# q and k of a tile, and V of two tiles, side by side for each partition: transfers that fill 64 partitions with 4 KB rows

## The chip, the cores and the metric

The kernel runs on one core of a Trainium2 chip. The metric is the device time of one execution in microseconds (us); several executions are timed and their median is taken. One more execution is recorded by the hardware profiler, and everything below that speaks of rows, waits and the chain comes from that one.

The core's engines are named as the profile names them: PE (matrix multiplies), PEld (PE's weight loads), DVE (vector), ACT (scalar, activations), POOL (GpSimd) and SP (which only issues transfers here). SBUF is the on-chip memory of 128 partitions, PSUM the memory that PE writes. Transfers (DMAs) between the off-chip memory and SBUF are carried by 16 DMA engines.

## The reference

Block-diagonal attention on 8 batches, 8 heads, 576 positions and 64 values per head, in chunks of 64, followed by a mixture of experts in which each token that passes a gate goes to one of eight experts:

```python
q_c = q.reshape(B, H, nc, chunk, D)            # chunk = 64, k_c and v_c alike
scores = scale * np.matmul(q_c, k_c.transpose(0, 1, 2, 4, 3))
attn = np.exp(scores - np.max(scores, axis=-1, keepdims=True))
attn = attn / (np.sum(attn, axis=-1, keepdims=True) + 1e-09)
out = np.matmul(attn, v_c)
x = out.transpose(0, 2, 1, 3).reshape(B * S, H * D)      # 4608 tokens of 512 values
do_compute = x @ w_skip > 0
e_idx = argmax(x @ w_gate); gate = softmax(x @ w_gate)[e_idx]
result = x, and where do_compute: x + gate * (relu(x @ w1[e_idx]) @ w2[e_idx])
```

## The kernel before, in words

The 4608 tokens form 36 tiles (NT) of 128 tokens; a tile holds two chunks of all eight heads. The kernel has two stages. The first is the attention stage, a loop over `i` of 39 iterations (line 724 on) in which the steps of several tiles are interleaved by hand: in iteration `i` PE makes the scores of tile `i` (`pe_scores`, line 241), transposes the probabilities of tile `i - 2` (`pe_ptrans`, 273), multiplies those of tile `i - 3` with V (`pe_pv`, 289), transposes the result of tile `i - 4` (`pe_xt`, 316) and, every second iteration, makes the gate's logits of two tiles (`pe_logit`, 328). ACT copies PSUM to SBUF and takes exponentials, DVE takes the maxima and normalises, POOL subtracts. Beside these the routing of tokens to experts is counted, and the first expert's weights are loaded and split into two 16-bit parts. The second stage is the mixture of experts: rows are gathered by an indirect transfer from POOL, multiplied by two weight matrices and scattered back.

The transfers of the attention stage are all issued by SP, in the order in which the code names them. Three kinds bring the inputs:

- `load_q(t)` (line 126) and `load_k(t)` (129) each fill one half of the tile `st`, 128 partitions with 512 fp32 values each, so 2048 bytes a row and 256 KB a transfer. The inputs were laid out by the host so that these are whole blocks of memory.
- `load_v(t)` (133) fills a tile `sv`: 128 partitions, 520 values (2080 bytes) each, 260 KB. The values carry a column of ones that gives the softmax's sum.

The first five tiles of q and k (`QK_AHEAD`) and the first six of V (`V_AHEAD`) are loaded ahead of the loop. In iteration `i` the loop issues `load_q(i + 5)` right after the scores of tile `i`, then one transfer of `side` (line 304: a result tile written to `out`, line 310, or half a weight chunk `wst`, line 360), later `load_v(i + 3)` and `load_k(i + 5)`. There are five `st` buffers and six `sv` buffers, so `load_q(i + 5)` waits until PE has read tile `i`'s scores inputs, and `load_v(i + 3)` until PE has read V of tile `i - 3`.

Nobody plans this order at run time: within an engine the instructions stand as the code was recorded, and between engines semaphores hold. Each SP transfer uses one of eight completion semaphores in turn and waits for the transfer that used it before, so that at most eight SP transfers are under way.

Of the kernel before, what the change touches and what calls it, by code (L numbers as in the profile page):

```python
# [9 lines left out]
F32 = mybir.dt.float32  # L10
# [8 lines left out]
P = 128  # L19
B, H, S, D = 8, 8, 576, 64  # L20
CH = 64
NTOK = B * S
NT = NTOK // P
# [3 lines left out]
KC = DM // P  # L27
# [28 lines left out]
QK_AHEAD = 5  # L56
V_AHEAD = 6
# [46 lines left out]
def moe_attention_kernel(ctx: ExitStack, tc: tile.TileContext, qk: bass.AP, vo: bass.AP, cst: bass.AP, crow: bass.AP, wall: bass.AP, out: bass.AP):  # L104
    nc = tc.nc
# [8 lines left out]
    ap = apool.__enter__()  # L114
# [5 lines left out]
    T = [dict() for _ in range(NT)]  # L120
    lgs = {}
    halves = (slice(0, CH), slice(CH, P))

    def load_q(t):
        T[t]["st"] = ap.tile([P, 2, DM], F32, name="st", bufs=QK_AHEAD)
        nc.sync.dma_start(T[t]["st"][:, 0], qk[0, t])

    def load_k(t):
        nc.sync.dma_start(T[t]["st"][:, 1], qk[1, t])

    def load_v(t):
        T[t]["sv"] = ap.tile([P, 2 * KC, D + 1], F32, name="sv", bufs=V_AHEAD)
        nc.sync.dma_start(T[t]["sv"].rearrange("p h d -> p (h d)"), vo[t])

    man = tc.manual_schedule()
    man.__enter__()
    csb = cpool.tile([P, CCOLS], F32, name="csb")
    rsb = cpool.tile([1, RCOLS], F32, name="rsb")
    for t in range(QK_AHEAD):
        load_q(t)  # L140
        load_k(t)
        if t == 1:
            nc.sync.dma_start(csb, cst)
        if t == 2:
            nc.sync.dma_start(rsb, crow)
        if t >= 2:
            load_v(t - 2)
    for t in range(QK_AHEAD - 2, V_AHEAD):
        load_v(t)
# [8 lines left out]
    def pe_warm(n):  # L158
        for _ in range(n):
            nc.tensor.matmul(warm, ones, zeros, start=True, stop=True)  # L160
# [32 lines left out]
    def more_constants():  # L193
        nc.vector.tensor_copy(upper, C("upper"))
        nc.vector.tensor_copy(cbase, C("cbase"))
        nc.vector.tensor_copy(recs[:, 0:2], C("tok").rearrange("p (c t) -> p c t", c=2))
        nc.vector.tensor_copy(dcon, csb[:, _C["wdesc"][0]:_C["iota"][1]])
        nc.vector.memset(ecum[:, 0, :], 0.0)
        nc.vector.memset(onesf, 1.0)
# [28 lines left out]
    def fill(q, budget):  # L228
        while q and budget >= 0.5 * q[0][0]:
            c, _, f = q.pop(0)  # L230
            f()
            budget -= c
# [59 lines left out]
    def ve_x(t):  # L292
        xq = T[t].pop("xq")[:, :, :XW].rearrange("p a (j d) -> p a j d", j=KC)
        rr = spool.tile([P, 2, KC, 1], F32, name="rr", bufs=2)
        nc.vector.tensor_scalar(rr, xq[:, :, :, D:], 1e-9, None, op0=ALU.add)
        nc.vector.reciprocal(rr, rr)
        x = ap.tile([P, DM], F32, name="xa", bufs=X_BUFS)
        nc.vector.tensor_tensor(x.rearrange("p (j a d) -> p a j d", a=2, d=D), xq[:, :, :, :D], rr.to_broadcast([P, 2, KC, D]), op=ALU.mult)  # L298
        rows.append((t, x))
        T[t]["x"] = x  # L300
# [3 lines left out]
    def side(i, n):  # L304
        for _ in range(n):
            if pieces and (pieces[0] < FC and i in W_AT or i >= BURST and pieces[0] >= FC and (not rows or pieces[0] <= (i - BURST) * 2 + FC)):
                load_half(pieces.pop(0))
            elif rows:
                t, x = rows.pop(0)
                nc.sync.dma_start(out[t * P:(t + 1) * P, :], x)  # L310
# [52 lines left out]
    def conv_half():  # L363
        st, hi, lo = cws.pop(0)
        nc.scalar.activation(hi, st, AF.Copy, scale=SW)
        fd.append((600, None, lambda: nc.vector.scalar_tensor_tensor(lo, st, SW, hi, op0=ALU.mult, op1=ALU.subtract)))

    def pool_lo():
        hi, st, lo = pl.pop(0)
        nc.gpsimd.tensor_tensor(lo, st, hi, op=ALU.subtract)  # L370
# [271 lines left out]
    def on(f, t):  # L642
        if 0 <= t < NT:
            f(t)
# [26 lines left out]
    def stage(g):  # L671
        next(jobs[g])
# [27 lines left out]
    def u0_mm():  # L700
        fc, n = u0[0], units[0][3]
        u0[0] += 1
        hp = u0_bank(fc)[:, :n]
        for m, (a, b, j) in enumerate((a, b, j) for a, b in ((0, 0), (0, 1), (1, 0)) for j in range(KC)):
            nc.tensor.matmul(hp, wsets[0][:, a, fc, j * P:(j + 1) * P], xt0[:, b, j, :n], start=(m == 0), stop=(m == 11))
        u0_ev.append((hp, fc))

    def u0_out():
        l1_out(ht0, *u0_ev.pop(0), units[0][3])

    def early_xt():
        return [blk_xt(xt0[:, :, :, m * P:(m + 1) * P], xgs[m], xp=u0_bank(m)) for m in range(2)]

    def do(i, spot):
        for f, a in spots.pop((i, spot), ()):
            f(*a)

    def conv_pool():
        st, hi, lo = cws.pop(0)
        nc.scalar.activation(st, st, AF.Copy, scale=SW)  # L720
        nc.scalar.activation(hi, st, AF.Copy)
        pl.append((hi, st, lo))

    for i in range(NT + 3):
        on(pe_scores, i)
        on(load_q, i + QK_AHEAD)
        if i == 2:
            more_constants()
        wm = WARM[i + 1] if i + 1 < len(WARM) else (0, 0, 0, 0)
        pe_warm(wm[0])  # L730
        on(ve_max, i - 1)
        if i != NT + 1:
            on(ve_x, i - 4)
        side(i, 1 if i < BURST else 2)
        if i % 2 == 0:
            on(ve_logit, i - 8)
        do(i, "d")
        if i == NT + 1:
            for f in lows:
                f()  # L740
        fill(fd, 600)
        do(i, "p")
        pe_warm(wm[1])
        on(ac_scores, i)
        on(pe_ptrans, i - 2)
        on(ac_pt, i - 2)
        do(i, "m")
        on(ac_exp, i - 1)
        pe_warm(wm[2])
        while pl:  # L750
            pool_lo()
        for c in range(W_CONV.count(i)):
            conv_half() if i < NT - 2 else conv_pool()
        pe_warm(wm[3])
        on(pe_pv, i - 3)
        if i >= 3:
            on(load_v, i - 3 + V_AHEAD)
        on(load_k, i + QK_AHEAD)
        if i >= BURST:
            side(i, 2)  # L760
        if i == NT + 2:
            ve_x(NT - 1)
            stage(5)
        if i % 2 == 0:
            on(pe_logit, i - 6)
            on(ac_logit, i - 6)
        if i % 2:
            on(pe_ltrans, i - 7)
        on(pe_xt, i - 4)
        on(ac_xt, i - 4)  # L770
        do(i, "e")
        if i == NT:
            ve_x(i - 3)
            scpool.__exit__(None, None, None)
            upool = tc.tile_pool(name="ps_u", bufs=1, space=PSUM, reuse_waits="tile")
            ps_u = upool.__enter__()
            lows = early_xt()
        if i > NT:
            u0_mm()
        if u0_ev and i > NT + 1:  # L780
            u0_out()
# [214 lines left out]
def lay_out(q, k, v, moe_w_skip, moe_w_gate, moe_w1, moe_w2):  # L996
    nch = S // CH

    def cols(a):
        a = a.reshape(B, KC, 2, nch, CH, D).transpose(0, 3, 5, 1, 2, 4).reshape(NT, 2, D, KC, 2, CH).copy()  # L1000
        a[:, :, :, :, 1] = a[:, ::-1, :, :, 1]
        return a.reshape(NT, P, DM)

    vv = v.reshape(B, KC, 2, nch, CH, D).transpose(0, 3, 2, 4, 1, 5).reshape(NT, 2, P, KC, D).transpose(0, 2, 1, 3, 4)
    vo = np.ones((NT, P, 2, KC, D + 1), np.float32)
    vo[..., :D] = vv
    vo = vo.reshape(NT, P, 2 * KC * (D + 1))
    qk = np.ascontiguousarray(np.stack([cols(q), cols(k)]))
    cst, crow = constants()
    wsg = np.concatenate([moe_w_skip[:, None], moe_w_gate], axis=1)  # L1010
    lo, hi = _C["wsg"]
    wp = np.zeros((P, KC, WP), np.float32)
    wp[:, :, :NE + 1] = wsg.reshape(KC, P, NE + 1).transpose(1, 0, 2)
    cst[:, lo:hi] = wp.reshape(P, -1)
    w1 = moe_w1.reshape(NE, KC, P, FC, P).transpose(0, 3, 2, 1, 4).reshape(NE, FC, P, KC * P)
    w2 = moe_w2.reshape(NE, FC, P, DM)
    wall = np.ascontiguousarray(np.concatenate([w1, w2], axis=3))
    return {"in_qk": qk, "in_vo": vo, "in_cst": cst, "in_crow": crow, "in_wall": wall}
# [14 lines left out]
```

## Time and profile before

| what | value |
|---|---|
| median of 3 runs | 351.37 us (349.95 to 352.65) |
| the profiled execution's own time | 348.98 us |
| its span | 347.1 us |
| PE, DVE, ACT, POOL busy | 94%, 69%, 56%, 37% of the span |
| moved by DMA | 81.85 MB, 62.2% of the 16 engines' span in SP's queue |
| first and last score matmul | 5.7 and 118.5 us after the span's start |

The profile has several views. The page gives busy shares, the span in 40 equal slices (each digit is the busy share in tenths), the DMA queues, the chain of work that ended last and the costliest groups. The trace behind it can be asked for windows (busy time of each engine, the granted clock of PE, the mean busy share of the 16 DMA engines and the GB/s that they moved in a stretch of time), for waits (who waited for whom, total, how often, longest), for the chain of waits in order of time, and for a timeline. In a row of the timeline stand the start, the duration, the engine and line, the operation, the tile written and the tiles read, and a count. A packet is counted whole in the window in which it starts, so a share can come out a little above 1. "issue" means that the engine waited for nothing that the profile shows.

### The profile page before, as it was taken

What the parts mean: (1) busy time and instruction counts of PE and PEld (TensorE: products, weight loads), DVE (VectorE), ACT (ScalarE), POOL (GpSimd) and SP (SyncE); (2) the same over time, 40 slices, a digit from 0 to 9 for tenths busy, and PEclk for the clock granted to TensorE, in tenths of its full rate; (3) what the DMA queues carried; (4) which work ended last, traced back from release to release, by engine and by line L of the source; (5) the groups of instructions that cost most, each with busy time, mean ns of one, the idle gap of its engine ahead of it and who ended that gap; (6) DMA issues with size and microseconds to landing.
All of it is one profiled execution on the core that took longest, in us unless ns stands there. A gap on an engine that the chain in (4) does not pass through costs nothing.

```text
span 347.1 us, 10869 instructions
## 1 busy us (share of the span) xinstructions
PE 325.1 (94%) x4364; PEld 223.3 (64%) x4364; DVE 239.7 (69%) x534; ACT 194.7 (56%) x345; POOL 129.3 (37%) x158
## 2 busy tenths in 40 slices
PE   7699999998989899969999999999999999999991
PEld 3477777676767668638655555756756658678570
DVE  1545788876888787957787756966957948767430
ACT  2578889796778795414455633544634634636120
POOL 4523364543628466744143027316324222111111
PEclk9989999999999999999999999999999999999998
DMA  7999999999899981083558667668549667655000
GB/s 253 390 371 386 348 374 337 340 315 309 273 307 312 355 297 63 2 298 112 188 187 289 193 242 223 223 196 271 171 182 295 222 227 245 196 203 148 34 24 30
DMA packets 34407, 81.85 MB, mean 236 GB/s; under 512 B 4255, under 2 KB 4256, under 8 KB 34354
## 3 DMA queue, kind: packets, MB, share of 16 engines
q1 hardware_dynamic: 31250, 71.79, 62.2%
q0 software_dynamic: 3104, 9.33, 7.4%
q8 instruction: 36, 0.59, 0.7%
q14 instruction: 17, 0.14, 0.1%
HBM read 67.07 MB, written 14.17 MB: 234 GB/s over the span
## 4 chain that ended last, share of the span: by engine, by line
PE 79%; ACT 7%; DVE 5%; issue 4%; DMA 2%; POOL 2%; POOLq 0%; DVEq 0%; ACTq 0%
PE sp L544 26%; PE hp L519 23%; PE sc L241 7%; PE sp L316 5%; PE xq L289 4%; PE sp L273 4%; PE sp L328 3%; PE xt L502 2%; ACT sc L246 2%; ACT pz L278 2%; PE rk L160 2%; DMA xg<-out,rec3i 2%; PE xq L341 1%; POOL wset L370 1%; DVE x L552 1%
## 5 line engine op out<-in xcount | busy, mean ns | idle before, releaser
L544 PE MATMUL sp<-wset,ht 128*128 128x512 f16 (+7 forms) x528 | 104.0, 379 | 0.0
L519 PE MATMUL hp<-xt,wset 128*128 128x288 f16 (+6 forms) x768 | 85.8, 273 | 0.2 <-DVE ht L528 0.2
L519 PEld LDWEIGHTS <-wset 128*128 128x128 f16 x768 | 69.5, 98 | 17.3 <-issue 2.1
L544 PEld LDWEIGHTS <-ht 128*128 128x128 f16 (+7 forms) x528 | 46.6, 102 | 45.4 <-issue 1.7
L218 DVE SCALAR_TENSOR_TENSOR wset<-wst,wset 128x1024 f16<-128x1024 f32 x56 | 67.3, 1217 | 8.7 <-ACT wset L217 7.5
L221 POOL DMA_INDIRECT out<-x,recsi x18 | 23.6, 1310 | 112.9 <-DVE x L552 98.3
L253 POOL TENSOR_TENSOR px<-sc,mx 128x512 f32<-128x512 f32 x36 | 38.0, 1058 | 53.5 <-DVE mx L251 29.8
L217 ACT ACTIVATE wset<-wst 128x1024 f16<-128x1024 f32 x56 | 57.5, 1048 | 0.0
L527 ACT ACTIVATE ht<-hp 128x288 f16<-128x288 f32 (+6 forms) x64 | 24.4, 383 | 57.1 <-PE hp L519 56.0
L528 DVE SCALAR_TENSOR_TENSOR ht<-hp,ht 128x288 f16<-128x288 f32 (+6 forms) x64 | 26.0, 420 | 22.9 <-ACT ht L527 20.9
L251 DVE TENSOR_REDUCE mx<-sc 128x8 f32<-128x512 f32 x36 | 24.4, 678 | 19.0 <-ACT sc L246 18.5
L503 ACT ACTIVATE xt<-xt 128x512 f16<-128x512 f32 (+7 forms) x20 | 10.3, 513 | 47.5 <-PE xt L502 42.6
L241 PE MATMUL sc<-st 64*64 64x64 f32 x1152 | 27.3, 230 | 2.9 <-issue 2.1
L241 PEld LDWEIGHTS sc<-st 64*64 64x64 f32 x1152 | 21.9, 139 | 10.6 <-issue 6.3
L289 PE MATMUL xq<-sv,pz 64*64 64x65 f32 x1152 | 26.7, 228 | 1.9 <-issue 1.6
L246 ACT ACTIVATE sc<-sc 128x512 f32<-128x512 f32 x36 | 21.5, 597 | 11.2 <-PE sc L241 9.2
L289 PEld LDWEIGHTS xq<-sv,pz 64*64 64x64 f32 x1152 | 21.3, 137 | 8.7 <-issue 6.1
L273 PE MATMUL sp<-csb,px 128*128 128x128 f32 x144 | 24.0, 290 | 2.8 <-issue 2.8
L506 DVE SCALAR_TENSOR_TENSOR xt<-xt 128x512 f16<-128x512 f32 (+7 forms) x20 | 11.7, 585 | 21.4 <-ACT xt L503 18.2
L221 POOL DMA_INDIRECT xg<-out,recsi x18 | 24.3, 1352 | 5.5 <-issue 3.4
L322 ACT ACTIVATE xc<-sp 128x512 f32<-128x512 f32 x36 | 21.4, 595 | 8.1 <-PE sp L316 6.5
L298 DVE TENSOR_TENSOR xa<-xq,rr 128x512 f32<-128x512 f32 x36 | 24.9, 691 | 1.2
(156 smaller groups left out, 369.7 us busy)
## 6 DMA issues: line engine op xcount, KB each, us to landing
wst<-in_wall SPq DMA_DIRECT2D x56, 512.0 KB
st<-in_qk SPq DMA_DIRECT2D x72, 256.0 KB
sv<-in_vo SPq DMA_DIRECT2D x36, 260.0 KB
out<-xa SPq DMA_DIRECT2D x36, 256.0 KB
wst<-in_wall SPq DMA_DIRECT2D x16, 256.0 KB
csb<-in_cst SPq DMA_DIRECT2D x1, 312.5 KB
xg<-out,recsi POOLq DMA_INDIRECT x18
out<-x,recsi POOLq DMA_INDIRECT x18, 4.7
```

The costliest lines, as they stand in the source:

```text
L217: nc.scalar.activation(w[:, 0, fc, :], st, AF.Copy, scale=SW)
L218: nc.vector.scalar_tensor_tensor(w[:, 1, fc, :], st, SW, w[:, 0, fc, :], op0=ALU.mult, op1=ALU.subtract)
L221: ins = nc.gpsimd.indirect_dma_start(**kw)
L241: nc.tensor.matmul(sp[halves[c], a, j], st[halves[r], 0, w], st[halves[r], 1, w], start=(j == 0), stop=True, skip_group_check=True)
L246: nc.scalar.activation(sc.rearrange("p (j a) s -> p a j s", a=2), T[t].pop("sp"), AF.Copy)
L253: nc.gpsimd.tensor_tensor(px, T[t].pop("sc"), mx.unsqueeze(2).to_broadcast([P, H, CH]), op=ALU.subtract)
L273: nc.tensor.transpose(pt[:, j, :], px[:, j].rearrange("p a s -> p (a s)"), ident)
L289: nc.tensor.matmul(xq[w, a, j * (D + 1):(j + 1) * (D + 1)], pz[r, j, w], v[r, c, j], start=(j == 0), stop=True, skip_group_check=True)
L298: nc.vector.tensor_tensor(x.rearrange("p (j a d) -> p a j d", a=2, d=D), xq[:, :, :, :D], rr.to_broadcast([P, 2, KC, D]), op=ALU.mult)
L519: nc.tensor.matmul(hp, w()[:, a, fc, j * P:(j + 1) * P], xt[:, b, j, :n], start=(m == 0), stop=(m == 11))
L528: nc.vector.scalar_tensor_tensor(ht[:, 1, fc, :n], hp, 0.0, ht[:, 0, fc, :n], op0=ALU.max, op1=ALU.subtract)
L544: nc.tensor.matmul(y[c * P // cg:c * P // cg + n], ht[:, a, fc, o:o + n], w[:, b, fc, P * KC:], start=(f == 0 and m == 0), stop=(f == fw - ...
```

## The change

Nothing is computed otherwise. The host lays q and k of a tile side by side for each partition (1024 values, 4096 bytes), and V of tiles 2m and 2m + 1 side by side (1040 values, 4160 bytes). A transfer still moves 256 KB (260 KB for V), but now fills 64 of the 128 partitions with such rows: `load_qk0(t)` brings q and k of partitions 0 to 63, `load_qk1(t)` those of 64 to 127; `load_v(t)` brings, for an even `t`, V of tiles `t` and `t + 1` in partitions 0 to 63, and for an odd `t` the same two tiles' V in 64 to 127. The transfers stand at the same places of SP's order as the ones that they replace. V's six buffers of one tile become four of two tiles each (`V_AHEAD // 2 + 1`).

```diff
-    def load_q(t):
+    def load_qk0(t):
         T[t]["st"] = ap.tile([P, 2, DM], F32, name="st", bufs=QK_AHEAD)
-        nc.sync.dma_start(T[t]["st"][:, 0], qk[0, t])
-
-    def load_k(t):
-        nc.sync.dma_start(T[t]["st"][:, 1], qk[1, t])
+        nc.sync.dma_start(T[t]["st"][:P // 2], qk[t, :P // 2])
+
+    def load_qk1(t):
+        nc.sync.dma_start(T[t]["st"][P // 2:], qk[t, P // 2:])
 
     def load_v(t):
-        T[t]["sv"] = ap.tile([P, 2 * KC, D + 1], F32, name="sv", bufs=V_AHEAD)
-        nc.sync.dma_start(T[t]["sv"].rearrange("p h d -> p (h d)"), vo[t])
+        h = halves[t % 2]
+        if t % 2 == 0:
+            vp = ap.tile([P, 2, 2 * KC, D + 1], F32, name="sv", bufs=V_AHEAD // 2 + 1)
+            T[t]["sv"], T[t + 1]["sv"], T[t + 1]["vp"] = vp[:, 0], vp[:, 1], vp
+        else:
+            vp = T[t].pop("vp")
+        nc.sync.dma_start(vp[h].rearrange("p t h d -> p (t h d)"), vo[t // 2, h])
...
     for i in range(NT + 3):
         on(pe_scores, i)
-        on(load_q, i + QK_AHEAD)
+        on(load_qk0, i + QK_AHEAD)
...
         if i >= 3:
             on(load_v, i - 3 + V_AHEAD)
-        on(load_k, i + QK_AHEAD)
+        on(load_qk1, i + QK_AHEAD)
...
-    vo = vo.reshape(NT, P, 2 * KC * (D + 1))
-    qk = np.ascontiguousarray(np.stack([cols(q), cols(k)]))
+    vo = vo.reshape(NT // 2, 2, P, 2 * KC * (D + 1)).transpose(0, 2, 1, 3).reshape(NT // 2, P, 4 * KC * (D + 1)).copy()
+    qk = np.stack([cols(q), cols(k)], axis=2)
```

The diff adds five lines ahead of the rest, so that line 241 of the kernel before is line 246 after, and so on.

No engine's order changes but in shapes and waits. SP's queue in the first iterations of the loop, before: `st` is the tile of q and k, `sv` that of V, `xa` a result; DMAHW0 to DMAHW7 are the eight completion semaphores, and PE in a wait means that PE has to have read the buffer.

```order
L126 DMA st<-in_qk 128x512 [waits DMAHW0_49,PE_49]
L133 DMA sv<-in_vo 128x520 [waits DMAHW1_49,PE_49]
L129 DMA st<-in_qk 128x512 [waits DMAHW2_49]
L126 DMA st<-in_qk 128x512 [waits DMAHW3_49,PE_49]
L310 DMA out<-xa 128x512 [waits DMAHW4_49,DVE_49]
L133 DMA sv<-in_vo 128x520 [waits DMAHW5_49,PE_49]
```

The same place of SP's queue after:

```order
L126 DMA st<-in_qk 64x1024 [waits DMAHW0_49,PE_49]
L138 DMA sv<-in_vo 64x1040 [waits DMAHW1_49]
L129 DMA st<-in_qk 64x1024 [waits DMAHW2_49]
L126 DMA st<-in_qk 64x1024 [waits DMAHW3_49,PE_49]
L315 DMA out<-xa 128x512 [waits DMAHW4_49,DVE_49]
L138 DMA sv<-in_vo 64x1040 [waits DMAHW5_49]
```

The order stands; the shapes are 64 partitions by twice the columns, and V's transfers no longer wait for PE, since their buffer was last read an iteration earlier.

PE's queue where it makes scores, transposes probabilities and multiplies with V, from the scores of tile 5 on, before (`sc` are scores, `xq` is the product with V):

```order
L241 MATMUL sc<-st 64x64 [waits DMAHW3_49,DMAHW2_49,Activation_49]
L241 MATMUL sc<-st 64x64 x15
L273 MATMUL sp_405<-csb,px 128x128 [waits PE_49,Activation_49]
L273 MATMUL sp_405<-csb,px 128x128 x3
L289 MATMUL xq<-sv,pz 64x65 [waits DMAHW6_49,DVE_49,PE_49]
L289 MATMUL xq<-sv,pz 64x65 x15
```

And after:

```order
L246 MATMUL sc<-st 64x64 [waits DMAHW2_49,Activation_49]
L246 MATMUL sc<-st 64x64 [waits DMAHW3_49]
L246 MATMUL sc<-st 64x64 x14
L278 MATMUL sp_401<-csb,px 128x128 [waits PE_49,Activation_49]
L278 MATMUL sp_401<-csb,px 128x128 x3
L294 MATMUL xq<-sv,pz 64x65 [waits DMAHW6_49,DVE_49,PE_49]
L294 MATMUL xq<-sv,pz 64x65 [waits DMAHW7_49]
L294 MATMUL xq<-sv,pz 64x65 x14
```

Each score still waits for two transfers, now one after the other; the product with V of an even tile waits for two transfers where it waited for one, and that of the odd tile for none.

More of the change, by code (lines that the diff above doesn't have):

```diff
@@ L139, in moe_attention_kernel @@
     for t in range(QK_AHEAD):
-        load_q(t)
-        load_k(t)
+        load_qk0(t)
+        load_qk1(t)
         if t == 1:
```

## The prediction

> **What bounds the kernel now.** I read the page's slices first, then the stage that the change touches in windows of 10 us, then PE's waits and the chain in that stage. The slices (engines' busy tenths, DMA's, and GB/s):
>
> ```profile
> PE   7699999998989899969999999999999999999991
> ...
> DMA  7999999999899981083558667668549667655000
> GB/s 253 390 371 386 348 374 337 340 315 309 273 307 312 355 297 63 2 298 112 188 187 289 193 242 223 223 196 271 171 182 295 222 227 245 196 203 148 34 24 30
> ```
>
> A slice is 8.7 us. In the first 15, the attention stage, PE and the DMA engines are both full; nothing else of the kernel is touched. Two windows there (busy us of PE, PEld, DVE, ACT, POOL, then PE's clock, DMA share, GB/s):
>
> ```profile
> 20.00:30.00 10.00, 9.88 (x268) 7.58 (x266) 6.10 (x15) 8.37 (x15) 3.13 (x3) 0.99 1.03 374
> 30.00:40.00 10.00, 9.76 (x270) 7.31 (x270) 5.88 (x14) 8.65 (x17) 3.13 (x3) 1.00 1.03 375
> ```
>
> Which of the two is late? PE's waits, longest first and the last row (who waits, for whom, us in total, times, longest):
>
> ```profile
> PE xt L502 <- DMA xg<-out,rec3i: 3.2, 1, 3.2
> PE sp L273 <- issue: 2.8, 1, 2.8
> ...
> PE xq L289 <- PE sp L273: 0.2, 1, 0.2
> ```
>
> The one DMA that PE waits for is a gather of the second stage; no row names `st` or `sv`. The chain of waits repeats every two tiles with PE and ACT alone, which the transposition of the logits' inputs marks:
>
> ```profile
> 24.98 0.64 PE sp L328 x8
> ...
> 30.81 0.64 PE sp L328 x8
> ...
> 36.64 0.64 PE sp L328 x8
> ```
>
> So two tiles take 5.83 us of PE and ACT, 2.92 us each, and transfers just keep up. They have no room: a cheaper transfer shortens nothing, a dearer one soon shows.
>
> **Price of a transfer by its bytes.** A stretch with rows of 2 KB alone, and one of the second stage with the 4 KB rows of the weights alone, both over 128 partitions:
>
> ```profile
> 9.80:11.80 2.00, 1.97 (x53) 1.24 (x43) 1.29 (x3) 1.58 (x4) 1.32 (x2) 1.00 1.05 402
> 149.90:151.40 1.50, 1.50 (x11) 0.76 (x8) 1.27 (x4) 0.60 (x1) 0.33 (x1) 1.00 1.02 415
> ```
>
> GB/s by share is the rate of full engines: 402/1.05 = 383 and 415/1.02 = 407. 262,144 bytes then take 0.68 us now and 0.64 us with 4 KB rows: 0.04 us less for each. That is the whole gain, and the chain above does not contain it.
>
> **Price of filling half of the partitions.** No transfer of before fills 64 partitions. The nearest rows are the last scatters of expert rows from SBUF, one row of 2 KB for each partition, of 128, 104 and 112 rows (`BLOCKS`, line 50), issued by POOL
>
> ```profile
> 324.88 0.99 POOL L221 DMA_INDIRECT out<-x,recsi  x1 [11.05 <-DVE x L552]
> 331.55 1.02 POOL L221 DMA_INDIRECT out<-x,recsi  x1 [5.67 <-DVE ht L528]
> 341.48 0.96 POOL L221 DMA_INDIRECT out<-x,recsi  x1 [8.91 <-issue]
> ```
>
> with nothing else under way 1.6 us later, in the same order:
>
> ```profile
> 326.50:327.00 0.50, 0.50 (x4) 0.29 (x3) 0.23 (x1) 0.00 (x0) 0.00 (x0) 1.00 1.00 377
> 333.30:333.55 0.25, 0.25 (x7) 0.15 (x4) 0.25 (x2) 0.01 (x1) 0.00 (x0) 1.00 1.16 213
> 343.00:343.40 0.40, 0.00 (x0) 0.00 (x0) 0.00 (x0) 0.00 (x0) 0.00 (x0) 1.00 1.05 287
> ```
>
> Rates of full engines: 377 for 128 rows, 213/1.16 = 184 for 104, 287/1.05 = 273 for 112. Engines are as busy and move 2.05 and 1.38 times less. I read it so: over 128 partitions each engine has a way into SBUF of its own, and where the partitions are not all there, two engines are sent through one. That reading is an inference, these rows read SBUF where the change writes it, and they are short; but they are the only rows here in which partitions are missing.
>
> If 64 partitions give the 16 engines half of the ways, a transfer costs between 0.64 us (factor 1) and 1.32 us (factor 2.05). It need not be the whole factor, because the transfers alternate between lower and upper partitions: when one of two engines that share a way is ahead, it is already in the other half and both run freely. How far are they apart? The first transfer's first packets:
>
> ```profile
> 2.04:2.20 0.16, 0.16 (x2) 0.08 (x1) 0.00 (x0) 0.16 (x1) 0.16 (x2) 1.00 0.49 141
> 2.20:2.36 0.16, 0.16 (x2) 0.07 (x1) 0.00 (x0) 0.01 (x1) 0.16 (x1) 1.00 0.64 230
> 2.36:2.48 0.12, 0.12 (x1) 0.00 (x0) 0.00 (x0) 0.00 (x0) 0.12 (x1) 1.00 0.93 358
> ```
>
> Half of the engines start at 2.04 us, the rest by 2.48, on average about 0.28 us later. If the early and the late engine share a way and keep that lead, each transfer saves it: 1.32 - 0.28 = 1.04 us. I take that value, since full engines stay as far apart as they started; the ends 0.64 and 1.32 stay for the range.
>
> **Who must wait for it.** SP's issues up to the last one for q and k, of tile 35, by line (duration in ns, first and last start):
>
> ```profile
> L126 SPq DMA_DIRECT2D st<-in_qk x36: 327/328/975, 0.7 to 101.8; - x36
> L129 SPq DMA_DIRECT2D st<-in_qk x36: 328/441/1554, 1.2 to 103.4; - x36
> L133 SPq DMA_DIRECT2D sv<-in_vo x34: 327/328/1019, 4.4 to 103.0; - x34
> L310 SPq DMA_DIRECT2D out<-xa x19: 344/382/1917, 18.7 to 102.2; - x19
> L360 SPq DMA_DIRECT2D wst<-in_wall x8: 422/423/1572, 42.4 to 88.8; - x8
> L143 SPq DMA_DIRECT2D csb<-in_cst x1: 432/432/432, 2.6 to 2.6; - x1
> ```
>
> That is 36 + 36 + 34 = 106 transfers that change, 27 of 256 KB that don't (0.68 us each, 18.4) and the constants (312.5 KB, 0.8 us), from 2.0 us on. At a price P the last scores can start at 106 P + 18.4 + 0.8 + 2.0 = 106 P + 21.2. They start now at
>
> ```profile
> 118.04 0.68 PE L241 MATMUL sc<-st 64*64 64x64 f32 x29
> ```
>
> With P = 0.64 the transfers are through at 89 us, 29 us early. The point from which they decide is P = (118.0 - 21.2)/106 = 0.91. With 1.04 the scores start at 131.4, 13.4 us late. The same sum at tile 20, with 61 changed transfers and 12 others ahead of it in SP's order, and now
>
> ```profile
> 65.19 0.69 PE L241 MATMUL sc<-st 64*64 64x64 f32 x32
> ```
>
> gives 61 x 1.04 + 8.2 + 2.8 = 74.4 against 65.2, 9 us late: the delay builds up through the stage and is no matter of its end. After tile 35 the same work of PE follows as now, so the delay stays: **+13 us**.
>
> **The other edits.** V's transfer of an even slot no longer waits for PE; SP's waits on that line now:
>
> ```profile
> SPq L133 <- PE xq L289: 8.9, 13, 1.8
> ...
> SPq L133 <- PE xq L341: 4.2, 6, 1.1
> ```
>
> 13 us of SP's time go, but PE does not wait for V, so it is worth nothing; if engines are the bound, the wait for the transfer eight places earlier comes in its place. V of an even tile needs both halves, the second issued one iteration later. It is issued four iterations, about 12 us, before its use; at P = 1.04 eight transfers need 8.3 us. Nothing, then; without that cover it would be one transfer for each pair, 18 x 1.04 = 19 us at most. `load_qk1` adds no wait: q and k were both needed before. No instruction of PE, DVE, ACT or POOL is added.
>
> **Sum.** 348.98 us of the profiled execution + 13 = 362; the median lies 2.4 us above that execution, which is itself below the lowest of the three runs, so I say **363 us**.
>
> **The rivals.**
>
> *Ways are shared and no lead helps.* The engines drain, restart together, and lower and upper transfers run one after the other at half rate: P = 1.32, last scores at 161, +43 us, 394. For it: the full 2.05 of the 104 rows. Against: the spread at the start. [...] Chance 0.14.
>
> *The price stays under the point of 0.91.* Writes into SBUF may be taken in by something in between, so that a stretch of 0.6 us in the lower half is still written while the engine fills the upper, or the factor is the 1.38 of the 112 rows (P = 0.89). Then PE and ACT still set the pace, 349 to 353 us. For it: 29 us of room at P = 0.64, and rows that only show reads. Chance 0.32.
>
> *Faster.* Transfers do set the pace somewhere, for the share of 1.03 says so; each of 106 saves 0.04 us, 4 us in all, 345 us by the profiled execution, 347 by the median. It decides if P stays at 0.64 and the stretches that the profile names "issue" are late data. Against: no wait of PE for `st` or `sv`. Chance 0.10.
>
> **How the numbers follow.** The forecast, P from 0.95 to 1.2, has 0.44; its own range is +4 to +30 us, 355 to 381. A measurement of this kernel tells about 1% (3.5 us) from no change. Faster by more: the last rival and a little chance, 0.11. Within: the rival under the point and the weak end, 0.30. Slower: forecast and first rival, 0.59. The range runs from 346 to 384; it leaves out the first rival and the edge of the last, together under 0.2.
>
> **What would show it.** Right: waits of PE for `st` at line 246 of some 13 us together, DMA share still about 1.0 between 20 and 100 us but 260 to 300 GB/s instead of 374, last scores near 131 us, and the second stage as long as now. First rival: 200 to 230 GB/s and last scores near 160. Second: GB/s and the 5.83 us of two tiles unchanged. Third: shorter than 5.83 us. The forecast is wrong if the rate of full engines stays near 400 GB/s, or if the delay shows up without waits for `st` or `sv`.

## The result, and the profile after

The changed kernel takes 391.25 us (median of 4, 387.5 to 396.8) against 350.87 us; the ratio is 1.111 with a 95% interval of 1.101 to 1.121. It is 40 us slower, where 12 were forecast: outside the range, and three times the forecast. A few executions of each kernel come out longer than the rest (396.8 is one), and ratios compare the others.

The profiled execution took 387.5 us with a span of 385.7. The page's slices (9.6 us each) of the changed kernel:

```profile
PE   7748797867797697999699999999999999999992
...
DMA  7999999999999999620815587586755876675100
GB/s 187 221 228 254 291 330 244 254 259 257 242 239 232 271 327 360 247 83 2 306 26 206 184 294 215 175 286 188 220 207 184 298 237 206 213 229 190 44 24 27
```

The DMA engines are as full as before and for longer, but move 220 to 330 GB/s in most slices where they moved 270 to 390. Two windows of the changed kernel (PE, PEld, DVE, ACT, POOL, PE's clock, DMA share, GB/s):

```profile
20.00:30.00 10.00, 5.47 (x109) 4.25 (x109) 2.44 (x5) 3.12 (x6) 1.48 (x2) 0.80 1.04 230
...
60.00:70.00 10.00, 8.35 (x226) 6.31 (x228) 6.43 (x20) 6.84 (x14) 4.82 (x11) 1.00 1.04 244
```

The first of these stood at 374 GB/s with PE at 9.88 us busy. What PE waits for, in the changed kernel:

```profile
PE sc L246 <- issue: 10.1, 7, 2.7
PE xq L294 <- issue: 8.5, 5, 2.9
PE sc L246 <- DMA st<-in_qk: 7.1, 7, 3.4
PE xt L507 <- DMA xg<-out,rec3i: 3.2, 1, 3.2
PE sp L278 <- issue: 2.9, 1, 2.9
PE sp L321 <- issue: 1.8, 1, 1.8
```

Waits for `st` are new, as forecast, but only 7 us stand under that name, and all seven end before 27 us. Idle time put down to "issue" grew from 6.5 to 24 us; asked for 28 to 154 us alone, the view has rows of "issue" and no other. From the scores of tile 6 to those of tile 35 PE does the same 2296 matrix multiplies, before and after:

```profile
22.95:118.04 95.09, 89.98 (x2296) 68.11 (x2295) 73.37 (x216) 76.52 (x144) 46.78 (x68) 0.98 0.98 333
31.14:153.81 122.67, 97.18 (x2296) 72.80 (x2295) 73.28 (x220) 76.82 (x143) 45.78 (x67) 0.94 1.02 275
```

It takes 27.6 us longer: 20.4 us more idle, and 7.2 us more busy at a granted clock of 0.94 instead of 0.98. The end of the stage in the changed kernel, from SP's last load of q and k (tile 35) to the scores that use it:

```profile
136.69 0.59 SPq L129 DMA_DIRECT2D st<-in_qk  x1
...
140.93 2.31 SPq L315 DMA_DIRECT2D out<-xa  x3
...
153.81 0.69 PE L246 MATMUL sc<-st 64*64 64x64 f32 x32
```

The load and the scores stood at 103.4 and 118.0. So the last load is issued 33 us later and its scores start 36 us later; the rest of the kernel, 231.9 us of the span, took 229.1 before, so 3 us more. All of the loss but that is in the attention stage.

The row in the middle tells when that load was there. At most eight of SP's transfers are under way, so a transfer has landed when the eighth one after it is issued. For the load of tile 35 that is the last of the three, at 142.8 us: 11 us before its scores. By the same count each load of q and k from tile 10 on landed at least 6 us before its scores, and V some 10 us before its product.

### The profile page after: what moved, and what is told of

It is laid out like the page before. It is cut to its first block, busy times and chain, and to the rows that moved or that the text cites. A ratio compares the mean times of both kernels' runs of the same rounds, so it can differ in the third digit from the quotient of the medians.

```text
span 385.7 us, 10821 instructions
## 1 busy us (share of the span) xinstructions
PE 338.2 (88%) x4364; PEld 230.5 (60%) x4364; DVE 238.3 (62%) x534; ACT 195.1 (51%) x345; POOL 130.5 (34%) x158
## 4 chain that ended last, share of the span: by engine, by line
PE 72%; DMA 8%; issue 8%; ACT 5%; DVE 3%; POOL 1%; SPq 0%; POOLq 0%; DVEq 0%; ACTq 0%
PE sp L549 24%; PE hp L524 20%; PE sc L246 6%; PE sp L321 5%; PE xq L294 4%; DMA st<-in_qk 4%; PE sp L278 4%; PE sp L333 3%; PE xt L507 2%; DMA sv<-in_vo 2%; ACT pz L283 2%; DMA xg<-out,rec3i 2%; PE xq L346 1%; ACT sc L251 1%; POOL wset L375 1%
## 5 line engine op out<-in xcount | busy, mean ns | idle before, releaser
L549 PE MATMUL sp<-wset,ht 128*128 128x512 f16 (+7 forms) x528 | 106.6, 385 | 0.0
L246 PE MATMUL sc<-st 64*64 64x64 f32 x1152 | 31.4, 240 | 18.0 <-issue 10.1
L246 PEld LDWEIGHTS sc<-st 64*64 64x64 f32 x1152 | 24.6, 148 | 26.9 <-issue 18.2
L294 PE MATMUL xq<-sv,pz 64*64 64x65 f32 x1152 | 28.5, 235 | 8.7 <-issue 8.5
L294 PEld LDWEIGHTS xq<-sv,pz 64*64 64x64 f32 x1152 | 22.6, 143 | 16.1 <-issue 13.8
L278 PE MATMUL sp<-csb,px 128*128 128x128 f32 x144 | 25.2, 300 | 3.7 <-issue 2.9
L321 PE MATMUL sp<-csb,xa 128*128 128x128 f32 x144 | 24.7, 296 | 1.8 <-issue 1.8
L283 ACT ACTIVATE pz<-sp 128x512 f32<-128x512 f32 x36 | 21.5, 598 | 8.4 <-PE sp L278 7.6
```

Of the source, the lines that this page charges most:

```text
L246: nc.tensor.matmul(sp[halves[c], a, j], st[halves[r], 0, w], st[halves[r], 1, w], start=(j == 0), stop=True, skip_group_check=True)
L278: nc.tensor.transpose(pt[:, j, :], px[:, j].rearrange("p a s -> p (a s)"), ident)
L283: nc.scalar.activation(pz, T[t].pop("pt"), AF.Copy)
L294: nc.tensor.matmul(xq[w, a, j * (D + 1):(j + 1) * (D + 1)], pz[r, j, w], v[r, c, j], start=(j == 0), stop=True, skip_group_check=True)
L321: nc.tensor.transpose(xp[:, j, :], x[:, j * P:(j + 1) * P], ident)
L549: nc.tensor.matmul(y[c * P // cg:c * P // cg + n], ht[:, a, fc, o:o + n], w[:, b, fc, P * KC:], start=(f == 0 and m == 0), stop=(f == fw - ...
```

## The experiments

Five questions: is it the 64 partitions or the 4 KB rows; does V's pairing matter; what does such a transfer cost alone, and beside others; which 64 partitions; and was there room.

### q and k alone

```diff
 # the changed kernel, but V loaded and laid out as before
+        T[t]["sv"] = ap.tile([P, 2 * KC, D + 1], F32, name="sv", bufs=V_AHEAD)
+        nc.sync.dma_start(T[t]["sv"].rearrange("p h d -> p (h d)"), vo[t])
```

> q and k as in the changed kernel (64 partitions, 4 KB rows), V as before. The last scores of the changed kernel stand at 154 us, so by 106 P + 21.2 its price was P = 1.25 us. Theory A (half of the partitions give the 16 DMA engines half of the ways into SBUF, and the engines stay in step): 72 x 1.25 + 34 x 0.69 + 21.2 = 135, 17 us later than the 118 of before: about 368 us. Theory B (rows of 4 KB are dear, whatever they fill): the same 368. Theory C (V in pairs, of which the even tile needs two transfers, makes PE wait): 351, as before.

383.3 us, ratio 1.087 (1.076 to 1.099): 34 us slower, twice what theory A gave. That q and k alone lose much of it was expected by A and B (17 us); the size was not. Both took 1.25 us for a half, read back from the changed kernel through the prediction's sum; the first probe below gives 1.07.

### V alone

```diff
 # the kernel before, but V in pairs of tiles, 64 partitions a transfer
+        nc.sync.dma_start(vp[h].rearrange("p t h d -> p (t h d)"), vo[t // 2, h])
```

> V as in the changed kernel, q and k as before. Theory A: 34 x 1.25 + 72 x 0.68 + 21.2 = 113, under the 118 of before: 351 to 354 us. Theory B: the same. Theory C: most of the 40 us, 375 to 391.

The median is 379.1 us against 349.6; the two shortest executions took 374.6 and 376.3, some 26 us more. A and B said 0 to 3, so the sum that both use is wrong. C said 375 or more. But C's mark would be PE waiting at the product with V for the second half, and PE's waits in this kernel have no row for `sv`:

```profile
PE sc L246 <- issue: 9.1, 5, 3.0
PE xq L294 <- issue: 8.9, 6, 2.7
PE xt L507 <- DMA xg<-out,rec3i: 4.9, 1, 4.9
PE sc L246 <- DMA st<-in_qk: 4.7, 4, 2.3
```

The waits for q and k, which are loaded as before, all end before 18 us, and from the second pair on each second half of V landed at least 6 us before its product. What is left is "issue". In the windows the engines are full at a low rate, although three of four transfers fill 128 partitions (before: 348, 340 and 287 GB/s at shares of 1.00, 0.99 and 0.89):

```profile
40.00:50.00 10.00, 9.56 (x251) 7.44 (x252) 5.97 (x17) 8.12 (x15) 3.13 (x3) 1.00 1.04 298
60.00:70.00 10.00, 7.96 (x210) 6.19 (x210) 6.33 (x18) 6.92 (x13) 5.38 (x11) 1.00 1.06 293
80.00:90.00 10.00, 7.69 (x210) 5.88 (x204) 7.79 (x22) 7.10 (x13) 6.38 (x12) 1.00 1.05 261
```

So a few half transfers make the whole ones dear too. The second probe below measures that by itself.

### 4 KB rows over all partitions

```diff
 # the changed layout, one transfer for both halves
+        nc.sync.dma_start(T[t]["st"], qk[t])
+            nc.sync.dma_start(vp.rearrange("p t h d -> p (t h d)"), vo[t // 2])
```

> The changed layout, but one transfer of 512 KB over all 128 partitions in place of two halves, in the place of the first (V of a pair alike, in the even slot): rows of 4096 and 4160 bytes, half as many transfers. Theory A: rows cost 0.64 us for 256 KB and all ways are open, so PE and ACT set the pace: 348 to 352 us, DMA share below that of before. Theory B: 391, as the changed kernel. Theory C: V comes in pairs here too, but with one wait each: 351.

357.6 us, ratio 1.019 (1.010 to 1.028): no 391, so theory B falls; rows of 4 KB are not what costs. Theory C gave 351 here too and is not tested by this run; it falls by q and k alone, where it gave 351 and 383 was measured. But this kernel is 8 us slower than before, which no theory had. Two windows of this kernel show DMA engines that are not full in the stage:

```profile
40.00:50.00 10.00, 7.95 (x182) 5.76 (x174) 5.57 (x18) 5.29 (x11) 2.09 (x2) 0.83 0.82 304
60.00:70.00 10.00, 9.38 (x244) 6.98 (x237) 7.91 (x23) 8.15 (x17) 3.31 (x4) 1.00 0.90 304
```

The waits of its PE name "issue":

```profile
PE sc L243 <- issue: 5.6, 5, 1.9
PE xq L291 <- issue: 4.1, 4, 2.0
...
PE rk L414 <- issue: 1.9, 1, 1.9
...
PE sp L275 <- issue: 0.5, 1, 0.5
```

12 us against 6.5 before. The trace suggests what such a gap is. Packets of 16 KB of the kind "instruction" come on a DMA queue of their own (queue 8, 36 pieces), some 5 to 9 us apart in this stage, and each of these gaps ends 1.3 to 1.7 us after the end of one such packet: 43 gaps in four traces (the kernel before, the changed one, V alone, and this one). I take the packets for PE's code, which is inferred from these times alone.

### What a transfer costs alone

```diff
 # ahead of the changed kernel, eight scratch buffers b, 32 transfers a block
+        probe(32, lambda i, b: nc.sync.dma_start(b[:, :DM], flat(i, lo)))
+        probe(32, lambda i, b: nc.sync.dma_start(b[(lo, hi)[i % 2]], rows(i, (lo, hi)[i % 2])))
+        probe(32, lambda i, b: nc.sync.dma_start(b[lo], rows(i, lo)))
+        probe(32, lambda i, b: nc.sync.dma_start(b, qk[i].rearrange("p a d -> p (a d)")))
+        probe(32, lambda i, b: (nc.scalar if i % 2 else nc.sync).dma_start(b[(lo, hi)[i % 2]], rows(i, (lo, hi)[i % 2])))
```

> The changed kernel, with five blocks of 32 transfers into eight scratch buffers ahead of it, nothing else running: 256 KB over 128 partitions in rows of 2 KB; 256 KB alternating between partitions 0 to 63 and 64 to 127 in rows of 4 KB; the same into 0 to 63 alone; 512 KB over 128 partitions in rows of 4 KB; the second block again with the two halves issued by SP and ACT in turn. Rates in GB/s. Theory A: 385, 200, 200, 405, and the last open between 200 and 400. The prediction's lead of 0.28 us kept: 252 for the second block, 200 for the third. Theory B: 385, 200, 200, 200, 200. Theory C: 385, 405, 405, 405, 405.

One window from the middle of each block:

```profile
9.00:14.00 5.00, 0.00 (x0) 0.00 (x0) 0.00 (x0) 0.00 (x0) 0.00 (x0) 1.00 1.05 393
...
40.00:50.00 10.00, 0.00 (x0) 0.00 (x0) 0.00 (x0) 0.00 (x0) 0.00 (x0) 1.00 1.03 246
...
85.00:95.00 10.00, 0.00 (x0) 0.00 (x0) 0.00 (x0) 0.00 (x0) 0.00 (x0) 1.00 1.04 202
...
115.00:125.00 10.00, 0.00 (x0) 0.00 (x0) 0.00 (x0) 0.00 (x0) 0.00 (x0) 1.00 1.03 412
...
155.00:165.00 10.00, 0.00 (x0) 0.00 (x0) 0.00 (x0) 0.00 (x0) 0.00 (x0) 1.00 1.05 247
```

Nothing computes here, and the rates are 393 (128 partitions, 2 KB), 246 (halves in turn), 202 (lower half alone), 412 (128 partitions, 4 KB) and 247 (halves from two issuing engines). One half for itself runs at half of the rate of 412: 1.30 us for 256 KB. In turn they cost 262,144/246 = 1.07 us, so 0.23 us are saved by each change of halves, about the lead of the prediction (0.28); that a lead saves them is its reading, which the size fits and no run shows. Issuing from two engines changes nothing (247 against 246 GB/s).

### Shorter distances

If PE's code waits behind queued data, loads that run less far ahead might help. In three kernels:

```diff
-QK_AHEAD = 5
-V_AHEAD = 6
+QK_AHEAD = 3
+V_AHEAD = 4
```

> The changed kernel with loads of q and k three tiles ahead instead of five and of V four instead of six, so that fewer transfers stand in SP's queue; bytes, shapes and order inside an iteration stay. Theory F (PE's code, in 16 KB pieces, waits behind the data that is queued ahead of it, and 64-partition transfers make that queue slower to empty): PE's idle time put down to issue falls from 24 us to under 12, the time to 368 to 380 us. Theory A alone (the transfers themselves set the pace): 391 as before, or more, since a shallow queue loses the lead between engines.

> The kernel before with the same smaller distances. Theory F: the 6.5 us of idle time put down to issue fall to under 3 us, the time to 344 to 348. Theory A alone: no change, 349 to 351; if three tiles are too short a distance, PE waits for st and it is slower.

> 4 KB rows over all 128 partitions in transfers of 512 KB, with the same smaller distances. The kernel with the old distances took 357.6 us with 12 us put down to issue. Theory F: that falls under 4 us and the time to 346 to 351. Otherwise 357 stays, and its 8 us have another cause than code waiting behind data.

The changed kernel 388.1 us, ratio 1.098 (1.090 to 1.106); the kernel before 1.003 (0.999 to 1.007); 4 KB rows over all partitions 1.012 (1.005 to 1.019). Idle time put down to "issue" is 22 us in the first and 12 us in the third: neither falls much. The changed kernel is as slow with three fifths to two thirds of the distance, so what holds it is not how far the loads run ahead. Theory F is not borne out as its expectations put it, but the run does not empty the queue: the engines' share in the changed kernel stays at 1.03 or above in all but two of the 14 windows from 20 to 160 us, and between 20 and 140 us SP still waits 24 us for earlier transfers (36 us with the old distances). Whether code is late because the engines are full stays open.

### Halves with rows of 2 KB

```diff
 # the kernel before, q (and k alike) in two transfers of 128 KB
+        for h in halves:
+            nc.sync.dma_start(T[t]["st"][h, 0], qk[0, t, h])
```

> The kernel before with each transfer of q and k cut in two, partitions 0 to 63 and 64 to 127, rows of 2 KB as before and 128 KB each; V as before. If 64 partitions are what costs, whatever the rows: slower than before by 15 to 35 us, as with 4 KB rows in the same halves (383). If rows of 4 KB were needed for the loss: 349 to 353.

389.3 us, ratio 1.105 (1.097 to 1.112): slower with 2 KB rows too, and a little more than forecast. But its engines are not full in the stage:

```profile
20.00:30.00 10.00, 9.07 (x214) 6.86 (x214) 3.92 (x9) 5.82 (x11) 2.08 (x2) 0.83 0.76 213
60.00:70.00 10.00, 7.75 (x161) 5.96 (x160) 5.04 (x14) 4.48 (x9) 5.32 (x11) 0.83 0.91 267
```

At most eight transfers are under way, and here most are of 128 KB, which may be the reason; the run does not show it. Something else joins in, too: ACT waits for the weights that it splits in this stage, and PE waits 9.1 and 8.8 us for ACT.

```profile
ACT wset L367 <- DMA wst<-in_wall: 12.7, 4, 5.7
```

The changed kernel has no such row. The run shows that the rows need not be of 4 KB; it does not measure the halves' price.

### Which 64, and in what company

```diff
+        mid = slice(P // 4, 3 * P // 4)
+        probe(32, lambda i, b: nc.sync.dma_start(b[mid], rows(i, lo)))
+        probe(36, lambda i, b: half(i, b, (lo, lo, hi, hi)[i % 4]))
+        probe(36, lambda i, b: half(i, b, (lo, hi)[i // 4 % 2]) if i % 4 == 3 else whole(i, b))
+        probe(36, lambda i, b: whole(i, b) if i % 4 == 3 else half(i, b, (lo, hi)[(i - i // 4) % 2]))
```

> As the first probe, with four other blocks ahead of the changed kernel. First, 32 transfers of 256 KB in 4 KB rows into partitions 32 to 95: if 64 partitions as such are dear, 200 GB/s as into 0 to 63; if it matters which 64, because 0 to 63 and 64 to 127 each reach only half of the ways into SBUF and 32 to 95 reach all, 400. Second, halves in the order lower, lower, upper, upper: if engines keep a lead and save it once at each change of halves, 0.24 us for two transfers instead of for one, 262/1.18 = 222 GB/s against 247; without a lead 202. Third, three transfers of 128 partitions in 2 KB rows to one half: if only the half is dear (0.68 and 1.06 us), 336 GB/s; if halves slow the whole transfers beside them as V alone did in the kernel (0.97 us for all), 270. Fourth, three halves to one whole: 271 by the first reading, 248 by the second.

One or two windows from the middle of each of its four blocks:

```profile
15.00:20.00 5.00, 0.00 (x0) 0.00 (x0) 0.00 (x0) 0.00 (x0) 0.00 (x0) 1.00 1.03 408
...
40.00:50.00 10.00, 0.00 (x0) 0.00 (x0) 0.00 (x0) 0.00 (x0) 0.00 (x0) 1.00 1.04 216
...
80.00:90.00 10.00, 0.00 (x0) 0.00 (x0) 0.00 (x0) 0.00 (x0) 0.00 (x0) 1.00 1.05 274
90.00:95.00 5.00, 0.00 (x0) 0.00 (x0) 0.00 (x0) 0.00 (x0) 0.00 (x0) 1.00 1.06 254
...
115.00:125.00 10.00, 0.00 (x0) 0.00 (x0) 0.00 (x0) 0.00 (x0) 0.00 (x0) 1.00 1.05 240
```

The first row decides it. 64 partitions from 32 to 95, same rows, same size: 408 GB/s, as fast as 128 partitions (412) and twice as fast as 0 to 63 (202), with the 16 engines full in each case (1.03 to 1.04). It is not how many partitions a transfer fills but which. Beyond these rates no trace shows why.

Lower, lower, upper, upper runs at 216, between the 222 of a lead saved once for two transfers and the 202 without. Three whole transfers to one half run at 254 to 274, not at 336: 0.96 to 1.03 us for each of the four on average. Three halves to one whole, nearly the changed kernel's 106 to 27, run at 240: 1.09 us on average. The packets in the traces tell the two kinds apart. The 2 KB packets of whole transfers took 86 ns each by themselves, 126 ns beside one half in four and 147 ns beside three; added up over 16 engines that is 0.69, 1.01 and 1.18 us for a transfer. The 4 KB packets of halves make 1.08 us in turn by themselves, and 1.11 us in both mixtures. So it is the whole ones that become dear. By what path, no trace shows.

### Was there room?

```diff
+        if 3 <= i < 31:
+            nc.sync.dma_start(ap.tile([P, DM], F32, name="ex", bufs=4), wall[i % NE, i // NE, :, :DM])
```

> The kernel before with 28 more loads of 256 KB (128 partitions, 2 KB rows, from the weights into buffers that nobody reads), one in each of 28 iterations. If the transfers of before had the 29 us of room that the prediction gave them, 28 x 0.68 = 19 us more are hidden: 349 to 354. If they already set the pace or just keep it, each counts: 28 x 0.75 = 21 us, 366 to 372.

> The changed kernel with the same 28 loads. If its transfers set the pace, 28 x 0.93 us (what a transfer over 128 partitions costs there) = 26 us more: 412 to 420. If PE's code or PE's waits for each other set it and engines merely look busy: under 400.

In the kernel before the 28 loads cost 2.9% (1.9 to 4.0), 10 us, where room gave none and full engines gave 21: about half of their 19 us of engine time is hidden, half is not. That is no clean measure of the room of q, k and V: PE's waits for `st` are 2.8 us there, all before 21 us, while ACT waits 7.8 us for `wst` and PE 9 us for ACT. In the changed kernel they cost, by the profiled executions, 416.5 - 387.5 = 29 us, 1.04 us for each (the medians, 421.5 and 391.25, are 30 us apart): there each transfer counts in full, near the price of the mixture. That is what full engines would give; but ACT waits 25.8 us for `wst` in that run, so it does not tell by which path they hold PE.

## Why the prediction was wrong

**What bounds the kernel.** Right in the main: PE and ACT set the pace, transfers just keep up, and a dearer one shows. The 4 KB rows did what was said: 412 against 393 GB/s, 5% cheaper, and none of it reached the end.

**The price of a half transfer.** Right in size: 1.04 us was taken where the probe shows 1.07. Half the rate is there (202 GB/s for 0 to 63 against 408 for 32 to 95), and halves in turn save part of the loss (246). That two engines share a way, and that full ones stay as far apart as they started, are readings of the prediction that no run shows. In the changed kernel itself the packets up to 143 us make 1.08 us for a transfer of q and k and 1.00 us for one of V. The rival with a price under 0.91 falls with these rows.

**The sum.** One term was too small: "27 of 256 KB that don't (0.68 us each)". The packets of these transfers make 0.91 us in the changed kernel, with halves beside them. The prediction's own sum with the measured prices is 106 x 1.06 + 27 x 0.91 + 2.8 = 140 us where it gave 131.4, and the last load had landed by 142.8. So 6 us are this term and 2 us the changed transfers.

**The path from load to scores.** Here the prediction failed. Its step "At a price P the last scores can start at 106 P + 21.2" lets PE stand still for its loads until they come, and it named a delay without waits for `st` or `sv` as a sign of being wrong. That sign is there. PE waits 7.1 us for `st`, all of it before 27 us; of the 36 us that the last scores come later, 27.6 arise after the scores of tile 6, while q, k and V land ahead of their use, at least 3 us and from tile 10 on at least 6 us. There PE stands still in gaps that end 1.3 to 1.7 us behind a packet of the kind "instruction", 24 us against 4 in the same stretch before, and is 7 us longer busy at a lower clock (0.94 against 0.98). So the last scores start at 153.8, 11 us after their load has landed, where the sum has nothing between the two: of 22 us that they come later than forecast, about 8 are prices and 14 this path.

The "29 us early" of the same step compares a load with its user as well. The first half of tile 35 is issued at 135.0 us, when the scores of tile 30, begun at 133.2, have freed its buffer. The 14.6 us between the last load and its scores before, and the 17.1 us after, are therefore most of the time that PE takes for the five tiles between them. They are no measure of room, and how much there was is not shown.

Whether these packets are PE's code, and what delays them, is not shown either. It is likely that full engines do, for the 16 KB packets took 1.23 us on average in the stage against 1.07 before, and each transfer added to the changed kernel lengthens it by a whole transfer. But with 4 KB rows over all partitions 12 us of such gaps stand beside engines at 0.82 to 0.90 in the windows shown. What the data alone would have cost, had the code been in time, no run separates.

**The rivals.** "Ways are shared and no lead helps" gave 394 us, which is close to 391, by another mechanism: it needs 1.32 us for each half, and the probe shows 1.07 in turn. That it came out near is luck: its price, too high, makes up for the dearer whole transfers and the path that its sum lacks as well. Nor do halves in turn run as slowly as one half alone: 246 against 202 GB/s, 22% more. "Faster" is excluded.

**What would show it.** 260 to 300 GB/s was forecast between 20 and 100 us, and the eight windows there have 230 to 318, 264 on average: right. Last scores were forecast near 131 and start at 153.8. Of the 13 us of waits for `st`, 7 came, early in the stage; gaps under "issue" take the place of the rest and of more.

## What to carry to other kernels

Look at which partitions a transfer fills before looking at its rows: here 0 to 63 alone ran at 202 GB/s and halves cut at partition 64 in turn at 246, against 412 for all 128, and whole transfers became about as dear beside them (1.01 and 1.18 us instead of 0.69), while 64 partitions that span the middle cost nothing (408). Price a slower transfer by the mixture that it will run in, not by itself. And before a delay is charged to a load, compare when it landed with when its user started: here the loads were there, and PE stood still for something else.

## What was not expected of the hardware

- Three whole transfers (128 partitions, 2 KB rows) to one half ran at 254 to 274 GB/s, against 393 for whole ones alone: a quarter of halves takes a third of the rate, and the whole ones beside them become dear (1.01 us instead of 0.69).
- Transfers twice as large over all partitions, 512 KB with 4 KB rows, made the kernel 1.9% slower (1.0 to 2.8), although the probe moves them at 412 GB/s. Its idle time put down to "issue", gaps that end behind packets of the kind "instruction", is 12 us against 6.5. That this is the cause is likely by its size and not shown.
- SP's issue of a transfer of 64 partitions took 0.47 us at the median, that of the same bytes over 128 partitions 0.33 to 0.44 us, in the rows of the tiles' transfers.
